# Sigmoid attention and top-1 mixture of experts: leftover rows gathered as quarters of a row and turned by VectorE

## The chip, the cores and the metric

One core of a Trainium2 chip. The metric is the device time of one execution in microseconds; a lower time is better. The time of the kernel before is the median of three runs. One execution was also profiled, and all rows of a profile come from that one.

## The reference, cut to what matters

```python
# q, k, v: (8, 12, 448, 64) fp32; w_gate (768, 8); w1 (8, 768, 1024); w2 (8, 1024, 768)
scores = q @ k.T / sqrt(64) - log(448)             # for each batch and head
x = (sigmoid(scores) @ v).transpose(0, 2, 1, 3).reshape(3584, 768)
logits = x @ w_gate
expert = argmax(logits, axis=1)                    # one of 8 experts for each row
gate = softmax(logits)[row, expert]
out[row] = gate * (relu(x[row] @ w1[expert]) @ w2[expert])
```

The kernel must give the output of shape (3584, 768) in fp32. Which rows go to which expert is known only when the attention has been computed.

## The kernel before, in words

**Stages.** The attention runs batch by batch and writes its rows to `x_tok` in memory. Seven *blocks* of 448 rows (0 to 6) each take one expert's weights through both layers (`moe`). The rows that such a block cannot hold are *leftover rows*. For them the attention stage writes *records* (row number, gate) to the memory array `recs`, in lists of 256 for one expert each. A list is an *item*. Two items always run, written out in full, behind block 6: item 0 and item 1 (`large`; in names of weights they carry the numbers 7 and 8). Further items run in a loop on the chip whose count comes from the data; in the profiled execution it takes no turn.

**Products.** Each fp32 operand is split in a high and a low part, and each product is made of three. A block has 144 products of 128x448 in the first layer (L231, eight steps j of 18) and 144 in the second (L254, six groups of 24). An item has as many, of 128x256: its first layer in L947, its second in L963. In the first layer ScalarE makes the hidden high part with a relu (`hh` in a block, `hih` in an item) and VectorE the low part (`hl`, `hil`). `ps_moe` has two PSUM banks, so the first product of step j + 2 waits for the low part of step j. In the second layer of a block, VectorE multiplies with the gate (L267) and turns the result (L268).

**Weights.** A raw tile `wst` is loaded by SP (five ahead). ScalarE casts it to the high part (`w1h`, `w2h`, L150), and GpSimd, or VectorE where `wts.low` says so, subtracts to get the low part (`w1l`, `w2l`, L151). First-layer parts have three buffers a kind, second-layer parts five.

**Leftover rows.** SP loads an item's records, 256 row numbers, two to a partition (L908). Two gathers on GpSimd's queue (L888) bring 128 whole rows each to `xg`. A row lies in `x_tok` as four quarters of six pieces of 32 elements; ScalarE copies it into six strips of four pieces, the order that the products need (`sort_rows`, L912). Then TensorE turns 128x128 pieces with an identity, four into one PSUM bank (L928), ScalarE casts to the high part (L932) and VectorE subtracts to get the low part (L933). Three calls of `split_rows` make an item's six *strips*, each a high and a low tile of 128x256 (`xrs_0`: `by_raw` and `rxf`; `xrs_1`: `rxh` and `rxl`).

**Order.** In this part the order on each engine is the order of the code. `mo` is a generator that issues block 6's products one by one; `more(n)` issues n of them and `until(n)` all but n, so the code between two such calls stands in the queues between those products. Item 0's products are stepped by `run` in the same way, and item 1's strips are made between its first steps.

Of the kernel before, what the change touches and what calls it, by code (L numbers as in the profile page):

```python
# [9 lines left out]
F32 = mybir.dt.float32  # L10
# [3 lines left out]
U32 = mybir.dt.uint32  # L14
AF = mybir.ActivationFunctionType
ALU = mybir.AluOpType
AX = mybir.AxisListType

P = 128
# [5 lines left out]
def tile_sigmoid_attention_top1_moe(  # L25
# [18 lines left out]
    nc = tc.nc  # L44
    B, H, S, D = q.shape
    NT, DM = out.shape
# [3 lines left out]
    KD = DM // P  # L50
# [7 lines left out]
    x_tok = dram.tile([NT, DM], F32, name="x_tok")  # L58
# [11 lines left out]
    ident = const.tile([P, P], F32, name="ident")  # L70
# [15 lines left out]
    TL = 2 * P  # L86
# [118 lines left out]
    def store():  # L205
        if stores:
            n, d, i, ob = stores.pop(0)
            cols = slice(d * DW + i * DW // 4, d * DW + (i + 1) * DW // 4)
            put = nc.sync.dma_start(
                out_b[bass.ds(maps[n], 1)][:, :, :, cols].rearrange("o r j f -> (o r) j f"),  # L210
                ob.rearrange("p j s t -> p j (s t)")[32 * i : 32 * (i + 1)],
            )
            apart(put, stored.setdefault((d, i), []))
# [571 lines left out]
    wts = Weights([(lambda b=b: regs.get(b)) for b in range(B + 1)])  # L785
# [8 lines left out]
    def more(n):  # L794
        nonlocal left
        for _ in range(min(n, left)):
            next(mo)
            left -= 1

    def until(n):  # L800
        more(left - n)
# [9 lines left out]
    rest = ctx.enter_context(tc.tile_pool(name="rest", bufs=1))  # L811
    ps_x = ctx.enter_context(tc.tile_pool(name="ps_x", bufs=2, space=bass.MemoryType.PSUM))
    ps_m2 = ctx.enter_context(tc.tile_pool(name="ps_m2", bufs=4, space=bass.MemoryType.PSUM))
    SMALL = P // 2

    xg = rest.tile([P, 2, DM], F32, name="xg")
    xgs = rest.tile([TS, DM], F32, name="xgs")
    xts_s = rest.tile([P, KD * TS], F32, name="xts_s")
    w1s = rest.tile([P, KD, DF], F32, name="w1s")
    w2s = rest.tile([P, KF, DM], F32, name="w2s")  # L820
# [21 lines left out]
    gate_e(NS - 1)  # L842
    more(9)
    nc.vector.tensor_sub(few, few, big)
    for cleared in (xg[:, 0], xg[:, 1], xgs):
        more(9)
        nc.vector.memset(cleared, 0.0)
    until(330)
# [27 lines left out]
    recs_v = recs.rearrange("(i t p) w -> i p t w", t=2, p=P)  # L876
    recs_s = recs.rearrange("(i r) w -> i r w", r=TL)
    recs_2 = [rest.tile([P, 2, 2], U32, name=f"rec_{n}") for n in range(3)]
    rec_s = rest.tile([TS, 1, 2], U32, name="rec_s")

    def item_reg(i):
        return nc.sync.value_load(li[0:1, bass.ds(i, 1)], min_val=0, max_val=NI - 1)

    def expert_reg(i):
        return nc.sync.value_load(li[0:1, bass.ds(i + P, 1)], min_val=0, max_val=E - 1)

    def gather(to, idx):
        nc.gpsimd.indirect_dma_start(  # L888
            out=to,
            out_offset=None,  # L890
            in_=x_tok,
            in_offset=bass.IndirectOffsetOnAxis(ap=idx, axis=0),
            bounds_check=NT - 1,
            oob_is_err=False,
        )
# [8 lines left out]
            oob_is_err=False,  # L904
        )

    def get_rows(ireg, rec):
        nc.sync.dma_start(rec, recs_v[bass.ds(ireg, 1)].rearrange("o p t w -> (o p) t w"))  # L908
        return [lambda t=t: gather(xg[:, t, :], rec[:, t, 0:1]) for t in range(2)]

    def sort_rows(to, frm):
        nc.scalar.copy(  # L912
            to.rearrange("p (k i s) -> p k i s", i=4, s=32), frm.rearrange("p (i k s) -> p k i s", i=4, s=32)
        )

    def sort_large(at, between=0):
        xp = [w2s[:, at + t] for t in range(2)]
        for t in range(2):
            sort_rows(xp[t], xg[:, t])
            more(between)  # L920
        return xp

    def split_rows(xp, xrs, k2):
        px = ps_x.tile([P, 512], F32, tag="px", name=f"px_{k2}")
        for kk in range(2):
            for t in range(2):
                at = kk * TL + t * P
                nc.tensor.transpose(px[:, at : at + P], xp[t][:, (2 * k2 + kk) * P : (2 * k2 + kk + 1) * P], ident)  # L928
        for kk in range(2):
            xh, xl = xrs[2 * k2 + kk]  # L930
            part = px[:, kk * TL : (kk + 1) * TL]
            nc.scalar.copy(xh, part)  # L932
            nc.vector.tensor_sub(xl, part, xh.bitcast(F32))  # L933

    def large(wts, b, rec, xrs, tags, home):

# [36 lines left out]
    def put_rows(xo, h, rec, puts):  # L973
        apart(scatter(xo[h], rec[:, h, 0:1]), puts)
# [8 lines left out]
    def small_rows(ireg):  # L983
        nc.sync.dma_start(rec_s, recs_s[bass.ds(ireg, 1), 0:TS].rearrange("o r (t w) -> (o r) t w", t=1))
        return [lambda: gather(xgs, rec_s[:, 0, 0:1])]

    def small_load(ereg, n):
        if n < KD:
            nc.sync.dma_start(w1s[:, n], w1[bass.ds(ereg, 1), n * P : (n + 1) * P, :].rearrange("e p n -> (e p) n"))
        else:  # L990
            j = n - KD
            nc.sync.dma_start(w2s[:, j], w2[bass.ds(ereg, 1), j * P : (j + 1) * P, :].rearrange("e p n -> (e p) n"))

    def yield_all(steps):
        while True:
            try:
                next(steps)
            except StopIteration as done:
                return done.value
# [3 lines left out]
    def small_item():  # L1003
# [51 lines left out]
    count = bass.RuntimeValue.of_register_unchecked(  # L1055
        bass.RegisterHandles([v_.val for v_ in loaded]), min_val=1, max_val=SMALL
    )
    gets = [get_rows(item_reg(n), recs_2[n]) for n in range(2)]
    regs[NS], regs[B] = expert_reg(0), expert_reg(1)
    more(24)  # L1060
    for get in gets[0]:
        get()
        more(12)
    more(36)
    by_raw = xpool.tile([P, S // 32, KD, 32], F32R, tag="raw", bufs=1, name="by_raw")
    by_raw = by_raw.rearrange("p j t s -> p (j t s)")
    first = [by_raw[:, n * TL : (n + 1) * TL] for n in range(2 * KD - 2)]
    first += [xpool.tile([P, S], F32R, tag="xf", bufs=6, name=f"rxf_{n}")[:, :TL] for n in range(2)]
    xrs_0 = [first[2 * t : 2 * t + 2] for t in range(KD)]
    xp_0 = sort_large(2, 12)  # L1070
    for get in gets[1]:
        more(12)
        get()
    for k2 in range(KD // 2):
        more(14)
        split_rows(xp_0, xrs_0, k2)
    more(24)
    xp_1 = sort_large(4, 12)
    until(24)
    wts.low = nc.vector  # L1080
    more(24)
    next(mo, None)
    xrs_1 = [
        [xpool.tile([P, S], F32R, tag=tag, name=f"r{tag}_{t}")[:, :TL] for tag in ("xh", "xl")] for t in range(KD)
    ]
    per_layer = 3 * KD * KF

    def run(steps, n):
        for _ in range(n):
            next(steps)  # L1090

    item = large(wts, NS, recs_2[0], xrs_0, (0, 2, 4), by_stores)
    for n in range(4):
        run(item, 20)
        store()
        if n < KD // 2:
            split_rows(xp_1, xrs_1, n)
    xo = yield_all(item)
    puts = []
    item = large(wts, B, recs_2[1], xrs_1, (6, 0, 2), by_stores)  # L1100
# [7 lines left out]
    with tc.If(count > 1, preferred_fallthrough_block=False):  # L1108
        with tc.For_i(1, count) as i, tc.manual_schedule():
            ereg, e_s = expert_reg(i + 1), expert_reg(i + SMALL - 1)  # L1110
            for get in get_rows(item_reg(i + 1), recs_2[2]) + small_rows(item_reg(i + SMALL - 1)):
                get()
            xp = sort_large(2)
            for k2 in range(KD // 2):
                split_rows(xp, xrs_1, k2)
            for n in range(KD + KF):
                small_load(e_s, n)
            ys = yield_all(large(Weights([lambda: ereg]), 0, recs_2[2], xrs_1, (0, 2, 4), by_hidden))
            for h in range(2):
                put_rows(ys, h, recs_2[2], [])  # L1120
            yield_all(small_item())
# [30 lines left out]
```

## Time and profile before

| | us |
|---|---|
| median of three runs | 781.88 (781.56 to 783.02) |
| time of the profiled execution | 784.5 |
| its span on the core | 782.7 |

| stretch of the span | from | to |
|---|---|---|
| block 6, first layer | 643.86 | 673.77 |
| block 6, second layer | 673.77 | 704.40 |
| item 0 | 704.40 | 740.24 |
| item 1 | 740.24 | about 775 |

The granted TensorE clock was 0.997 of full speed. PE is TensorE's products, PEld its weight loads, DVE is VectorE, ACT ScalarE, POOL GpSimd and SP the engine that issues most transfers. In a row of a timeline the first number is the start in microseconds, the second the duration, then engine, line, operation, output and inputs, shape, and the number of instructions that the row stands for; in brackets how long the engine idled before it and what released it. In a row of groups the numbers behind the bar are busy microseconds in all and mean nanoseconds of one. Names of tiles stand without their numbers.

### The profile page before, as it was taken

How to read it: one execution, taken by the hardware profiler on the slowest of the kernel's cores; microseconds unless marked ns; L12 is line 12 of the kernel's file. 1: busy time of each engine (PE TensorE's matmuls, PEld its weight loads, DVE VectorE, ACT ScalarE, POOL GpSimd, SP SyncE). 2: the span in 40 equal slices, each digit the busy share in tenths (PEclk: the TensorE clock that was granted, in tenths of full speed). 3: DMA queues.
4: the chain of work that ended last, by engine and by line, in shares of the span. 5: the costliest groups of instructions: out<-in, count | busy, mean ns of one | idle time of the engine just before them, and what ended most of it. 6: DMA issues, size and time to landing. Idle time of an engine off the chain costs nothing. (4 is left out here: it accounts for less than half of the span.)

```text
span 782.7 us, 15733 instructions
## 1 busy us (share of the span) xinstructions
PE 771.5 (99%) x5682; PEld 606.6 (78%) x5682; DVE 376.0 (48%) x811; ACT 384.9 (49%) x688; POOL 349.3 (45%) x331
## 2 busy tenths in 40 slices
PE   9999999999999999999999999999999999999996
PEld 5756556687686786867967769678688999999995
DVE  2354574375254652537425474244746492235443
ACT  5877675635536455264444552545523333435351
POOL 8747554152342332531615406054255755654341
PEclk9999999999999999999999999999999999999998
DMA  9776798975757847587576876766267555656661
GB/s 203 174 160 152 178 246 188 213 187 120 166 125 173 199 112 167 140 183 165 121 186 92 187 168 149 175 177 153 57 165 163 162 149 130 186 147 165 200 203 38
DMA packets 313683, 125.70 MB, mean 161 GB/s; under 512 B 210062, under 2 KB 311102, under 8 KB 313600
## 3 DMA queue, kind: packets, MB, share of 16 engines
q1 hardware_dynamic: 307552, 112.42, 61.5%
q0 software_dynamic: 5760, 11.76, 5.4%
q8 instruction: 47, 0.77, 0.4%
q10 hardware_dynamic: 288, 0.46, 0.2%
q14 instruction: 36, 0.29, 0.1%
HBM read 102.49 MB, written 22.49 MB: 160 GB/s over the span
## 5 line engine op out<-in xcount | busy, mean ns | idle before, releaser
L596 ACT ACTIVATE at<-sc,bias_s 128x448 f32<-128x448 f32 x336 | 193.4, 634 | 109.2 <-PE sc L610 108.1
L151 POOL TENSOR_TENSOR w1l<-wst,w1h 128x768 fp32r<-128x768 f32 x72 | 132.7, 1851 | 176.2 <-ACT w1h L150 161.7
L610 PE MATMUL sc<-qt,kt 64*64 64x448 f32 x1344 | 172.3, 546 | 1.1 <-ACT at L596 0.6
L627 PE MATMUL av<-at,vn 64*64 64x448 f32 x1344 | 168.6, 537 | 0.7 <-ACT xf L642 0.7
L151 POOL TENSOR_TENSOR w2l<-wst,w2h 128x512 fp32r<-128x512 f32 x84 | 106.9, 1298 | 138.6 <-ACT w2h L150 118.1
L610 PEld LDWEIGHTS sc<-qt,kt 64*64 64x64 f32 x1344 | 83.0, 189 | 56.1 <-issue 40.6
L231 PE MATMUL ps<-xh,w1h 128*128 128x448 f32 x336 | 124.3, 370 | 0.2 <-DVE nw L430 0.2
L231 PE MATMUL ps<-xh,w1l 128*128 128x448 f32 x336 | 123.4, 367 | 0.0
L231 PE MATMUL ps<-xl,w1h 128*128 128x448 f32 x336 | 123.3, 367 | 0.0
L254 PE MATMUL ps<-hh,w2l 128*128 128x448 f32 x336 | 123.3, 367 | 0.0
L254 PE MATMUL ps<-hl,w2h 128*128 128x448 f32 x336 | 123.2, 367 | 0.0
L254 PE MATMUL ps<-hh,w2h 128*128 128x448 f32 x336 | 122.7, 365 | 0.0
L627 PEld LDWEIGHTS av<-at,vn 64*64 64x64 f32 x1344 | 63.6, 133 | 59.9 <-issue 46.5
L150 ACT CAST w2h<-wst 128x512 fp32r<-128x512 f32 x108 | 64.6, 620 | 78.3 <-PE ps L254 64.5
L238 ACT ACTIVATE hh<-ps 128x448 fp32r<-128x448 f32 x56 | 30.6, 546 | 139.9 <-PE ps L231 139.9
L267 DVE TENSOR_TENSOR ps<-ps,gt 128x448 f32<-128x448 f32 x42 | 40.7, 969 | 85.9 <-PE ps L254 85.9
L486 DVE STREAM_TRANSPOSE xt<-av 128x448 f32<-128x448 f32 x48 | 28.5, 629 | 93.1 <-PE av L627 83.3
L239 DVE SCALAR_TENSOR_TENSOR hl<-ps,hh 128x448 fp32r<-128x448 f32 x56 | 34.4, 614 | 80.3 <-ACT hh L238 80.3
L231 PEld LDWEIGHTS ps<-xh,w1h 128*128 128x128 f32 x336 | 63.1, 188 | 9.9 <-issue 4.4
L254 PEld LDWEIGHTS ps<-hh,w2l 128*128 128x128 f32 x336 | 65.2, 194 | 6.6 <-issue 3.5
L254 PEld LDWEIGHTS ps<-hl,w2h 128*128 128x128 f32 x336 | 65.2, 194 | 6.2 <-issue 3.2
L254 PEld LDWEIGHTS ps<-hh,w2h 128*128 128x128 f32 x336 | 65.2, 194 | 3.4 <-DVE nw L430 0.2
(157 smaller groups left out, 953.8 us busy)
## 6 DMA issues: line engine op xcount, KB each, us to landing
wst<-in_moe_w_dram SPq DMA_DIRECT2D x72, 384.0 KB, 3.6
wst<-in_moe_w_dram SPq DMA_DIRECT2D x54, 512.0 KB, 5.0
x_tok<-xt SPq DMA_DIRECT2D x64, 168.0 KB, 2.9
qn<-in_q_dram SPq DMA_DIRECT2D x184, 56.0 KB, 3.5
raw<-x_tok SPq DMA_DIRECT2D x28, 336.0 KB, 8.1
out_dram<-ob SPq DMA_DIRECT2D x84, 112.0 KB, 2.3
kn<-in_k_dram SPq DMA_DIRECT2D x104, 56.0 KB, 4.4
kn<-in_k_dram POOLq DMA_DIRECT2D x80, 56.0 KB
```

What stands on the lines that cost most here:

```text
L150: nc.scalar.copy(hi, st)
L151: eng.tensor_tensor(lo, st, hi.bitcast(F32), op=ALU.subtract)
L231: nc.tensor.matmul(ps[:, :S], a[:, ws], b_, start=(t == 0 and n == 0), stop=(t == KD - 1 and n == 2))
L238: nc.scalar.activation(hh[:, :S], ps[:, :S], AF.Relu)
L239: nc.vector.scalar_tensor_tensor(hl[:, :S], ps[:, :S], 0.0, hh[:, :S].bitcast(F32), op0=ALU.max, op1=ALU.subtract)
L254: nc.tensor.matmul(ps[:, :S], a, b_, start=(j == 0 and n == 0), stop=(j == KF - 1 and n == 2))
L267: nc.vector.tensor_tensor(by_gate, by_gate, gate_rows[b], op=ALU.mult)
L486: nc.vector.transpose(xts[b][:, :, t, :], pv[:, :S].rearrange("p (j s) -> p j s", s=32))
L596: nc.scalar.activation(at, ps[:, :S], AF.Sigmoid, bias=bias_s, scale=SCALE)
L610: nc.tensor.matmul(ps[quarter(g, h), :S], ks, ops[g, "q"][OWN[h]], start=True, stop=True)
L627: nc.tensor.matmul(psv[g][OWN[h], :S], ops[g, "v"][rows, c, :], at[rows], start=(c == 0), stop=(c == KC - 1))
```

## The change

`x_tok` is seen as four times as many rows of 192 elements. A gather now brings 128 quarter rows: 32 rows, their four quarters in the four groups of 32 partitions. An item needs eight of them (`gather_quarters`, L915) in place of two gathers of whole rows. The index of a quarter is four times the row number plus the quarter's number; for that SP loads the row numbers four times, once for each group of partitions (L926), beside the record load that stays for the gate and the scatter (L930), and VectorE multiplies and adds (`place_rows`, L933, tile `at_q`). Rows that lie so need only a turn of blocks of 32x32 for a strip: one VectorE instruction into spare space of `w2s` (L942). ScalarE casts that to the high part (L944) and VectorE subtracts (L945), now with both inputs in SBUF. The 24 turning products and the four sorting copies of these two items are gone. `wts.low = nc.vector` stands earlier, so that all twelve second-layer low parts of block 6 are made by VectorE.

```diff
-    xg = rest.tile([P, 2, DM], F32, name="xg")
+    NB_I = TL // 32
+    xg = rest.tile([P, NB_I, KD, 32], F32, name="xg")
+    seg = rest.tile([P, 1], F32, name="seg")
+    for i in range(4):
+        nc.vector.memset(seg[32 * i : 32 * (i + 1)], float(i))
...
-    def get_rows(ireg, rec):
-        nc.sync.dma_start(rec, recs_v[bass.ds(ireg, 1)].rearrange("o p t w -> (o p) t w"))
-        return [lambda t=t: gather(xg[:, t, :], rec[:, t, 0:1]) for t in range(2)]
+    def gather_quarters(n, j):
+        nc.gpsimd.indirect_dma_start(
+            out=xg[:, j].rearrange("p t s -> p (t s)"),
...
+            in_=x_quarters,
+            in_offset=bass.IndirectOffsetOnAxis(ap=at_q[n][:, j : j + 1], axis=0),
...
+    def get_rows(ireg, n):
+        for i in range(4):
+            nc.sync.dma_start(
+                recs_q[n][32 * i : 32 * (i + 1)],
+                recs_s[bass.ds(ireg, 1)].rearrange("o (j r) w -> (o r) j w", r=32),
+            )
+        nc.sync.dma_start(recs_2[n], recs_v[bass.ds(ireg, 1)].rearrange("o p t w -> (o p) t w"))
+
+    def place_rows(n):
+        nc.vector.tensor_scalar(at_q[n], recs_q[n][:, :, 0], 4.0, seg, op0=ALU.mult, op1=ALU.add)
...
-    def split_rows(xp, xrs, k2):
-        px = ps_x.tile([P, 512], F32, tag="px", name=f"px_{k2}")
-        for kk in range(2):
-            for t in range(2):
-                at = kk * TL + t * P
-                nc.tensor.transpose(px[:, at : at + P], xp[t][:, (2 * k2 + kk) * P : (2 * k2 + kk + 1) * P], ident)
-        for kk in range(2):
-            xh, xl = xrs[2 * k2 + kk]
-            part = px[:, kk * TL : (kk + 1) * TL]
-            nc.scalar.copy(xh, part)
-            nc.vector.tensor_sub(xl, part, xh.bitcast(F32))
+    def split_rows(xrs, t):
+        whole = w2s[:, 2 + t, :TL]
+        nc.vector.transpose(whole.rearrange("p (j s) -> p j s", s=32), xg[:, :, t, :])
+        xh, xl = xrs[t]
+        nc.scalar.copy(xh, whole)
+        nc.vector.tensor_sub(xl, whole, xh.bitcast(F32))
...
-    gets = [get_rows(item_reg(n), recs_2[n]) for n in range(2)]
+    for n in range(2):
+        get_rows(item_reg(n), n)
     regs[NS], regs[B] = expert_reg(0), expert_reg(1)
     more(24)
-    for get in gets[0]:
-        get()
-        more(12)
+    wts.low = nc.vector
+    place_rows(0)
+    for j in range(NB_I):
+        more(5)
+        gather_quarters(0, j)
     more(36)
...
-    xp_0 = sort_large(2, 12)
-    for get in gets[1]:
-        more(12)
-        get()
-    for k2 in range(KD // 2):
-        more(14)
-        split_rows(xp_0, xrs_0, k2)
-    more(24)
-    xp_1 = sort_large(4, 12)
+    for t in range(KD):
+        split_rows(xrs_0, t)
+        more(8)
+    place_rows(1)
+    for j in range(NB_I):
+        more(5)
+        gather_quarters(1, j)
     until(24)
-    wts.low = nc.vector
...
         if n < KD // 2:
-            split_rows(xp_1, xrs_1, n)
+            split_rows(xrs_1, 2 * n)
+            split_rows(xrs_1, 2 * n + 1)
```

The same change stands in the loop for further items. Three places in the queues follow.

GpSimd's queue in block 6's first layer, before. `w1l_5` to `w1l_7` are the low parts for steps 5 to 7, `w2l_8` and on those of the second layer.

```order
L151 TENSOR_TENSOR w1l_5_7874<-wst_5_7620,w1h_5_7873 128x768
L888 DMA xg<-x_tok,rec_7765 128x768
L151 TENSOR_TENSOR w1l_6_7905<-wst_6_7640,w1h_6_7904 128x768
L888 DMA xg<-x_tok,rec_7765 128x768
L151 TENSOR_TENSOR w1l_7_7937<-wst_7_7668,w1h_7_7936 128x768
L151 TENSOR_TENSOR w2l_8_7943<-wst_8_7726,w2h_8_7942 128x512
```

The same queue now; `w1l_0` is item 0's first low part.

```order
L151 TENSOR_TENSOR w1l_5_7893<-wst_5_7625,w1h_5_7892 128x768
L915 DMA xg<-x_tok,at_q_7776 128x192 x2
L151 TENSOR_TENSOR w1l_6_7928<-wst_6_7645,w1h_6_7927 128x768
L915 DMA xg<-x_tok,at_q_7776 128x192 x3
L151 TENSOR_TENSOR w1l_7_7966<-wst_7_7673,w1h_7_7965 128x768
L915 DMA xg<-x_tok,at_q_7776 128x192 x3
L915 DMA xg<-x_tok,at_q_7777 128x192 x8
L151 TENSOR_TENSOR w1l_0_8275<-wst_0_8042,w1h_0_8274 128x768
```

Five gathers instead of two now stand ahead of `w1l_7`, and the second-layer low parts have left this queue.

VectorE's queue around the first gating of block 6's second layer, before. `hl_6` holds the low parts of steps 6 and 7.

```order
L239 SCALAR_TENSOR_TENSOR hl_6_8001<-ps_6_7_8014,hh_6_8000 128x448
L267 TENSOR_TENSOR ps_6_0_0_8037<-ps_6_0_0_8037,gt_7366 128x448
L268 STREAM_TRANSPOSE ob_0_8036<-ps_6_0_0_8037 128x448
L933 TENSOR_TENSOR by_raw<-px_8097,by_raw 128x256 x2
L267 TENSOR_TENSOR ps_6_0_1_8067<-ps_6_0_1_8067,gt_7366 128x448
```

The same place now.

```order
L942 STREAM_TRANSPOSE w2s<-xg 128x256
L945 TENSOR_TENSOR by_raw<-w2s,by_raw 128x256
L239 SCALAR_TENSOR_TENSOR hl_6_8035<-ps_6_7_8048,hh_6_8034 128x448
L942 STREAM_TRANSPOSE w2s<-xg 128x256
L945 TENSOR_TENSOR by_raw<-w2s,by_raw 128x256
L942 STREAM_TRANSPOSE w2s<-xg 128x256
L945 TENSOR_TENSOR by_raw<-w2s,by_raw 128x256
L942 STREAM_TRANSPOSE w2s<-xg 128x256
L945 TENSOR_TENSOR by_raw<-w2s,by_raw 128x256
L267 TENSOR_TENSOR ps_6_0_0_8076<-ps_6_0_0_8076,gt_7371 128x448
L268 STREAM_TRANSPOSE ob_0_8075<-ps_6_0_0_8076 128x448
```

One strip has moved ahead of the last `hl`, and three more stand between it and the first gating.

VectorE's queue in item 0's first layer, before. `psi_0` and `psi_1` are the sums of steps 0 and 1.

```order
L953 SCALAR_TENSOR_TENSOR hil_8330<-psi_0_8310,hih_8329 128x256
L933 TENSOR_TENSOR rxl_8299<-px_8343,rxh_8298 128x256
L933 TENSOR_TENSOR rxl_8301<-px_8343,rxh_8300 128x256
L953 SCALAR_TENSOR_TENSOR hil_8330<-psi_1_8339,hih_8329 128x256
L933 TENSOR_TENSOR rxl_8303<-px_8382,rxh_8302 128x256
```

The same place now.

```order
L965 SCALAR_TENSOR_TENSOR hil_8374<-psi_0_8354,hih_8373 128x256
L942 STREAM_TRANSPOSE w2s<-xg 128x256
L945 TENSOR_TENSOR rxl_8343<-w2s,rxh_8342 128x256
L942 STREAM_TRANSPOSE w2s<-xg 128x256
L945 TENSOR_TENSOR rxl_8345<-w2s,rxh_8344 128x256
L965 SCALAR_TENSOR_TENSOR hil_8374<-psi_1_8383,hih_8373 128x256
```

Each subtraction has got a turn ahead of it, and its input is `w2s` where it was the PSUM bank `px`.

More of the change, by code (lines that the diff above doesn't have):

```diff
@@ L844, in tile_sigmoid_attention_top1_moe @@
     nc.vector.tensor_sub(few, few, big)
-    for cleared in (xg[:, 0], xg[:, 1], xgs):
+    for cleared in (xg[:, : NB_I // 2], xg[:, NB_I // 2 :], xgs):
         more(9)
@@ L878, in tile_sigmoid_attention_top1_moe @@
     recs_2 = [rest.tile([P, 2, 2], U32, name=f"rec_{n}") for n in range(3)]
+    recs_q = [rest.tile([P, NB_I, 2], U32, name=f"rec_q{n}") for n in range(3)]
+    at_q = [rest.tile([P, NB_I], U32, name=f"at_q{n}") for n in range(3)]
+    x_quarters = x_tok.rearrange("n (i f) -> (n i) f", i=4)
     rec_s = rest.tile([TS, 1, 2], U32, name="rec_s")
@@ L905, in scatter @@
         )
-    def get_rows(ireg, rec):
-        nc.sync.dma_start(rec, recs_v[bass.ds(ireg, 1)].rearrange("o p t w -> (o p) t w"))
-        return [lambda t=t: gather(xg[:, t, :], rec[:, t, 0:1]) for t in range(2)]
+    def gather_quarters(n, j):
+        nc.gpsimd.indirect_dma_start(
+            out=xg[:, j].rearrange("p t s -> p (t s)"),
+            out_offset=None,
+            in_=x_quarters,
+            in_offset=bass.IndirectOffsetOnAxis(ap=at_q[n][:, j : j + 1], axis=0),
+            bounds_check=4 * NT - 1,
+            oob_is_err=False,
+        )
[4 more added lines that the diff above has]
+                recs_s[bass.ds(ireg, 1)].rearrange("o (j r) w -> (o r) j w", r=32),
+            )
+        nc.sync.dma_start(recs_2[n], recs_v[bass.ds(ireg, 1)].rearrange("o p t w -> (o p) t w"))
+    def place_rows(n):
+        nc.vector.tensor_scalar(at_q[n], recs_q[n][:, :, 0], 4.0, seg, op0=ALU.mult, op1=ALU.add)
     def sort_rows(to, frm):
@@ L914, in sort_rows @@
         )
-    def sort_large(at, between=0):
-        xp = [w2s[:, at + t] for t in range(2)]
-        for t in range(2):
-            sort_rows(xp[t], xg[:, t])
-            more(between)
-        return xp
-    def split_rows(xp, xrs, k2):
-        px = ps_x.tile([P, 512], F32, tag="px", name=f"px_{k2}")
-        for kk in range(2):
-            for t in range(2):
-                at = kk * TL + t * P
-                nc.tensor.transpose(px[:, at : at + P], xp[t][:, (2 * k2 + kk) * P : (2 * k2 + kk + 1) * P], ident)
-        for kk in range(2):
-            xh, xl = xrs[2 * k2 + kk]
-            part = px[:, kk * TL : (kk + 1) * TL]
-            nc.scalar.copy(xh, part)
-            nc.vector.tensor_sub(xl, part, xh.bitcast(F32))
+    def split_rows(xrs, t):
[4 more added lines that the diff above has]
+        nc.vector.tensor_sub(xl, whole, xh.bitcast(F32))
     def large(wts, b, rec, xrs, tags, home):
@@ L1110, in tile_sigmoid_attention_top1_moe @@
             ereg, e_s = expert_reg(i + 1), expert_reg(i + SMALL - 1)
-            for get in get_rows(item_reg(i + 1), recs_2[2]) + small_rows(item_reg(i + SMALL - 1)):
+            get_rows(item_reg(i + 1), 2)
+            place_rows(2)
+            for j in range(NB_I):
+                gather_quarters(2, j)
+            for get in small_rows(item_reg(i + SMALL - 1)):
                 get()
-            xp = sort_large(2)
-            for k2 in range(KD // 2):
-                split_rows(xp, xrs_1, k2)
+            for t in range(KD):
+                split_rows(xrs_1, t)
             for n in range(KD + KF):
```

## Prediction

> **What bounds the kernel now.** I read the page first, then the busy times by stretch over the part that changes, then each engine's timeline there.
>
> ```profile
> span 782.7 us, 15733 instructions
> PE 771.5 (99%) x5682; PEld 606.6 (78%) x5682; DVE 376.0 (48%) x811; ACT 384.9 (49%) x688; POOL 349.3 (45%) x331
> ```
> ```profile
> sum 131.00, PE 130.96 PEld 126.56 DVE 52.84 ACT 53.62 POOL 60.98; mean PE 32.74 PEld 31.64 DVE 13.21 ACT 13.41 POOL 15.25
> ```
>
> The sum is over 644 to 775 us: the last block (6), item 0 and item 1. TensorE idles 0.04 us of 131, so its queue is the clock: each product removed is time won, and each microsecond by which an operand comes too late is time lost, at once and in full. VectorE, ScalarE and GpSimd are under half busy, so only when their pieces end matters. I therefore walked the new order of every engine with the durations below and asked at each product of TensorE what is not there yet.
>
> **The gain.** Six groups of four turning products go.
>
> ```profile
> 678.05 0.37 PE L254 MATMUL ps<-hh,w2h 128*128 128x448 f32 x1
> 678.25 0.36 PE L254 MATMUL ps<-hl,w2h 128*128 128x448 f32 x1
> ...
> 681.71 0.36 PE L254 MATMUL ps<-hh,w2h 128*128 128x448 f32 x1
> 681.91 0.60 PE L928 MATMUL px<-ident,w2s 128*128 128x128 f32 x4
> 682.26 0.46 PE L254 MATMUL ps<-hl,w2h 128*128 128x448 f32 x1
> 682.56 0.36 PE L254 MATMUL ps<-hh,w2l 128*128 128x448 f32 x1
> ```
>
> From the product before a group (681.71) to the second behind it are 0.85 us; two pitches of 0.20 (first two rows) would be 0.41. A group costs 0.44, six cost **2.66 us**. The four sorting copies of ScalarE (0.83 each) lay in its idle time and give nothing.
>
> **Stall A: the eight gathers delay `w1l_7`.** Before, `w1l_6` and `w1l_7` had one gather ahead of each.
>
> ```profile
> 657.75 1.59 SPq L908 DMA_DIRECT2D rec<-recs  x2
> ```
> ```profile
> DMA to landing us min/median/max: 1.8/1.8/1.8
> ```
> ```profile
> 721.37 1.02 SPq L143 DMA_DIRECT2D wst<-in_moe_w_dram  x2
> ```
> ```profile
> 660.70 1.05 POOL L888 DMA_INDIRECT xg<-x_tok,rec  x1 [1.77 <-DVE hl L239]
> 661.77 1.86 POOL L151 TENSOR_TENSOR w1l<-wst,w1h 128x768 fp32r<-128x768 f32 x1
> 663.79 1.03 POOL L888 DMA_INDIRECT xg<-x_tok,rec  x1 [0.16 <-issue]
> 664.85 1.84 POOL L151 TENSOR_TENSOR w1l<-wst,w1h 128x768 fp32r<-128x768 f32 x1
> ...
> 674.15 1.02 POOL L888 DMA_INDIRECT xg<-x_tok,rec  x1
> 675.48 1.01 POOL L888 DMA_INDIRECT xg<-x_tok,rec  x1 [0.30 <-issue]
> ```
> ```profile
> 317.45 0.13 DVE L407 COPY rec<-gates 112x4 f32<-112x4 f32 x1
> ```
> ```profile
> 318.38 0.97 POOL L415 DMA_INDIRECT recs<-rec,si  x1 [2.93 <-DVE rec L407]
> ```
> ```profile
> 670.53 0.37 PE L231 MATMUL ps<-xh,w1l 128*128 128x448 f32 x1
> ```
>
> The records now come as four loads of 32 rows instead of one. Two plain issues of SP take 1.02, so 0.61 each with the tail; the fourth is issued 1.83 after the first (657.75), at 659.59. Landing takes at least 1.8; I take 2.06, the estimate that still leaves a wake-up of 0.80 before the gather at 660.70. So the records are there at 661.65. Now VectorE multiplies by 4 and adds the quarter (a small operation, 0.13 to 0.2): 661.85. A gather that waits for VectorE starts 0.80 after it (317.45 + 0.13 to 318.38): 662.65. Gather to gather is 1.33, gather to low part 1.06, low part to gather 0.16, a low part 1.85. Two gathers, `w1l_6`, three gathers, `w1l_7`: it starts at 670.79 and ends at 672.64 instead of 666.69, and TensorE wants it at 670.53. The old slack of 3.8 is gone; the stall is **2.1 us** (1.3 without the wake-up; 3.5 if SP needs 1.2 for each load, as in the 1.59 for two with their register work).
>
> **Stall B: the first pair of `item 0` stands ahead of block 6's last `hl`.** Gathers 6 to 8 go out behind `w1l_7`, at 672.80, 674.13 and 675.46. The turn needs all eight.
>
> ```profile
> q0 software_dynamic: 80, 0.39, 50.2%
> ```
> ```profile
> q0 software_dynamic: 80, 0.32, 18.3%
> ```
> ```profile
> 673.97 0.55 ACT L238 ACTIVATE hh<-ps 128x448 fp32r<-128x448 f32 x1 [1.34 <-PE ps L231]
> ```
> ```profile
> 674.55 0.62 DVE L239 SCALAR_TENSOR_TENSOR hl<-ps,hh 128x448 fp32r<-128x448 f32 x1 [3.02 <-ACT hh L238]
> ```
>
> The first two rows are the DMA queue of the gathers in 663.4 to 665.6 and in 665.6 to 670: the gather of 660.70 moved all its rows in the first, from 2.7 us after issue for about 2.1; that of 663.79 landed by 670. A quarter has a quarter of the bytes, 0.5. So a new gather lands 3.2 after issue, an estimate between 2.2 and 6.0 (663.79 to 670): 678.66. ScalarE's high part of the first strip stands ahead of the relu of j = 7, VectorE's turn and subtraction ahead of its `hl`: 0.40 + 0.37 + 0.55 + 0.60 = 1.92, at 680.58. TensorE wants that `hl` at 678.25 + 2.1 of stall A: **0.2 us** (0 to 2.6: microsecond for microsecond with the landing).
>
> The Trainium skill, page "DMA: Bandwidth & Descriptors", section "Anatomy of one DMA — SWDGE (gpsimd) path", puts such a transfer at about 2.0 us plus its bytes at 436 GB/s; by it a gather of 98 KB would land in an estimated 2.2 us and the sum would be about 1.0 lower, out of stalls B and C. The trace does not agree for the whole row: 2.9 us by that rule, 4.8 or more by the rows above.
>
> **Stall C: the strips in block 6's second layer.**
>
> ```profile
> L267 DVE TENSOR_TENSOR ps<-ps,gt 128x448 f32<-128x448 f32 x12 | 11.6, 966 | 19.6 <-PE ps L254 19.6
> L268 DVE STREAM_TRANSPOSE ob<-ps 128x448 f32<-128x448 f32 x12 | 7.8, 651 | 0.4
> ...
> L953 DVE SCALAR_TENSOR_TENSOR hil<-psi,hih 128x256 fp32r<-128x256 f32 x16 | 6.7, 420 | 12.9 <-ACT hih L952 12.9
> ...
> L933 DVE TENSOR_TENSOR rxl<-px,rxh 128x256 fp32r<-128x256 f32 x6 | 2.5, 425 | 3.2 <-ACT rxh L932 3.2
> ```
> ```profile
> L932 ACT CAST rxh<-px 128x256 fp32r<-128x256 f32 x6 | 2.2, 375 | 1.5 <-DVE rxl L933 1.5
> ```
>
> A strip is a turn (0.40, by size and a fixed part from L268's 0.65 at 448), a high part of 0.37 and a subtraction of 0.42, each waiting for the one before: 1.19. Three more strips now stand in VectorE's queue ahead of the first gating (0.97 + 0.65), the fifth ahead of `w2l_13`, the sixth ahead of `w2l_14`; ScalarE's high parts of the weights stand behind those of the strips. Walked from 680.58: `w2l_13` comes 0.2 late, `w2h_14` and `w2l_14` 0.45 and 0.3, and the second gating, behind them all, frees its bank 0.9 late: **1.85 us** (0.5 if the copies overlap better, 2.5 with the turns at the full 0.65).
>
> **Stall D: item 1's strips in item 0.** Two strips now stand between one `hil` and the next, three times.
>
> ```profile
> 708.16 0.42 DVE L933 TENSOR_TENSOR rxl<-px,rxh 128x256 fp32r<-128x256 f32 x1 [0.57 <-ACT rxh L932]
> ...
> 718.40 1.86 DVE L151 TENSOR_TENSOR w2l<-wst,w2h 128x512 fp32r<-128x512 f32 x1 [0.88 <-ACT w2h L150]
> ```
> ```profile
> 707.93 1.85 POOL L151 TENSOR_TENSOR w1l<-wst,w1h 128x768 fp32r<-128x768 f32 x1 [6.83 <-ACT w1h L150]
> ...
> 717.87 1.85 POOL L151 TENSOR_TENSOR w1l<-wst,w1h 128x768 fp32r<-128x768 f32 x1 [0.31 <-ACT w1h L150]
> ```
> ```profile
> 733.17 2.13 DVE L151 TENSOR_TENSOR w2l<-wst,w2h 128x512 fp32r<-128x512 f32 x3 [0.89 <-ACT w2h L150]
> ```
> ```profile
> 743.02 0.42 DVE L953 SCALAR_TENSOR_TENSOR hil<-psi,hih 128x256 fp32r<-128x256 f32 x1 [2.09 <-ACT hih L952]
> 745.18 0.42 DVE L953 SCALAR_TENSOR_TENSOR hil<-psi,hih 128x256 fp32r<-128x256 f32 x1 [1.74 <-ACT hih L952]
> ```
> ```profile
> 742.60 0.38 ACT L952 ACTIVATE hih<-psi 128x256 fp32r<-128x256 f32 x1 [5.82 <-PE psi L947]
> ```
> ```profile
> 743.79 1.84 POOL L151 TENSOR_TENSOR w1l<-wst,w1h 128x768 fp32r<-128x768 f32 x1 [0.43 <-ACT w1h L150]
> ```
>
> A low part on VectorE, both inputs in SBUF, takes 0.71 alone (2.13 for three) but 1.86 at 718.40, where GpSimd was in a low part until 719.72: it waited for its end. The old subtraction, one input in PSUM, ran its 0.42 inside GpSimd's 707.93 to 709.78. The new one has both inputs in SBUF. GpSimd's low part runs from 1.19 to 3.03 after a relu (742.60, 743.79). First strip after a relu: `hil` ends at 0.84, the turn 1.24, the high part 1.61; the subtraction waits for 3.03; then 0.42, the second strip 1.19, and the next `hil`, behind a relu that sits behind the second high part on ScalarE. From `hil` to `hil` that is about 4.05 us where TensorE's pitch is 2.16 (743.02 to 745.18). Two PSUM banks forgive the first 1.0; the rest is 0.86, 1.88 and 1.88, and `w2l_8` behind them 0.6: **5.2 us**. If the wait does not reach the subtraction, two strips of 1.19 and a `hil` of 0.42 are 2.8 against 2.16, and the banks take in nearly all: 0.6.
>
> The Trainium skill, page "SBUF — State Buffer", section "Who interferes with whom", states the same as a rule: a VectorE instruction with two SBUF inputs contends with a GpSimd instruction that reads SBUF, under an exclusive lock. By it the sum is the forecast, without it the first rival; the 1.86 against 0.71 agrees.
>
> **Costed at nothing.** The twelve second-layer low parts that move from GpSimd to VectorE are hidden in its idle half. Item 1's gathers follow on an empty GpSimd queue from about 690 and land before 706, ahead of their first turn near 708. SP's ten small loads push the raw second-layer weights back some 6 us; they still land at about 671.5, and no product waits for them. Four one-column memsets early on are below 1 us of idle VectorE.
>
> **The sum:** 2.1 + 0.2 + 1.85 + 5.2 − 2.66 = **+6.7 us**. On the profiled execution's 784.5 that is 791.2; the runs shown have the median 781.88, 2.6 lower, so I forecast **788.6**.
>
> **Rivals.** (1) *GpSimd does not hold the subtractions up.* For it: the rows of the wait are of 128x512, not 128x256. Against: the wait ended with GpSimd's instruction, whatever the size. Stall D is 0.6: +2.1, 784.0. (2) *All is hidden, the other side.* The walk's stalls A and B hang on issue times: if `w1l_7` is done by 670.53 (2.1 earlier, say with records after 1.8 and no wake-up), the gathers landed 2.2 after issue, and D without the wait, only the gain stays: −2.66, 779.2. The point that decides first is 670.53. Against: five gathers at 1.33 plus two low parts are 9.6 us behind a start that cannot be before 660.7. (3) *Gathers land late.* 4.5 to 6.0 after issue, as whole rows did: B grows by 1.3 to 2.8, to +9.5 or 791.4.
>
> **Chances.** Forecast 0.48, rival 3 0.16, both slower. Rival 1 0.24, of which 0.08 ends within 0.2% (1.56 us, about what a measurement of this kernel tells from no change) and 0.16 slower. Rival 2 0.12, 0.10 faster and 0.02 the same. So faster 0.10, same 0.10, slower 0.80. The range reaches down past rival 1's lower end (no wait, quick landings: −0.4), and up to rival 3 with the longer SP issues: 781.5 to 792.5. The forecast's own range is 786 to 791.
>
> **What would show it.** Right: a gap of about 2 us on TensorE near 671 before a product of `w1l`, small ones before `hl` near 680 and between 686 and 692, gaps of 1 to 2 us before three first products of item 0's first layer, and L945 at 1.0 to 1.8 us there instead of 0.42. Wrong: L945 at 0.42 throughout, `w1l_7` ending before 671, or a TensorE without gaps. Any gap in item 1 would be a cost that I have not seen.

## The result and the profile after

The changed kernel takes 792.74 us (median of four runs, 791.4 to 794.51) against 781.74: a ratio of 1.0132, 95% interval 1.0118 to 1.0147, or 9.2 to 11.5 us slower. The time lies 0.2 us above the top of the range, and the loss is larger than the 6.7 forecast. The profiled execution has 792.93 us and a span of 790.9.

The page's first line, and the sum of busy times over 644 to 783 us, the stretch that answers to 644 to 775 before:

```profile
span 790.9 us, 15757 instructions
```
```profile
sum 139.00, PE 131.62 PEld 123.64 DVE 69.87 ACT 50.45 POOL 59.14; mean PE 32.90 PEld 30.91 DVE 17.47 ACT 12.61 POOL 14.78
```

TensorE idled 0.04 us of this stretch before; now it idles 7.4. Its timeline shows where. These are the products behind a gap of more than 0.3 us; the bracket gives the idle time and what ended it.

```profile
672.33 0.47 PE L231 MATMUL ps<-xh,w1l 128*128 128x448 f32 x1 [1.15 <-POOL w1l L151]
...
680.58 0.48 PE L254 MATMUL ps<-hh,w2h 128*128 128x448 f32 x1 [0.46 <-ACT hh L238]
...
681.24 0.48 PE L254 MATMUL ps<-hl,w2h 128*128 128x448 f32 x1 [0.18 <-DVE hl L239]
...
689.89 0.48 PE L254 MATMUL ps<-hh,w2h 128*128 128x448 f32 x1 [0.22 <-ACT w2h L150]
...
693.59 0.46 PE L254 MATMUL ps<-hh,w2h 128*128 128x448 f32 x1 [0.66 <-DVE ob L268]
...
715.63 0.51 PE L959 MATMUL psi<-by_raw,w1h 128*128 128x256 f32 x2 [0.67 <-DVE hil L965]
...
719.63 0.50 PE L959 MATMUL psi<-by_raw,w1h 128*128 128x256 f32 x2 [1.58 <-DVE hil L965]
...
723.63 0.51 PE L959 MATMUL psi<-by_raw,w1h 128*128 128x256 f32 x2 [1.58 <-DVE hil L965]
```

The bracket leaves out the tail of the product before. Counted from start to start and less the usual pitch, the gaps are 1.31, 0.63, 0.46, 0.39, 0.83, 0.83, 1.74 and 1.74; with two of 0.2 in block 6's second layer, 8.3 us. Each stands within 2 us of where one of the four stalls was placed, with a releaser that the prediction named; only the gap before `hh` at 680.58 had no term of its own in the sum.

GpSimd's queue at stall A, now:

```profile
661.92 1.05 POOL L915 DMA_INDIRECT xg<-x_tok,at_q  x1 [2.81 <-DVE at_q L933]
663.27 1.01 POOL L915 DMA_INDIRECT xg<-x_tok,at_q  x1 [0.31 <-issue]
664.32 1.85 POOL L151 TENSOR_TENSOR w1l<-wst,w1h 128x768 fp32r<-128x768 f32 x1
666.33 1.30 POOL L915 DMA_INDIRECT xg<-x_tok,at_q  x1 [0.16 <-issue]
...
670.44 1.83 POOL L151 TENSOR_TENSOR w1l<-wst,w1h 128x768 fp32r<-128x768 f32 x1
...
675.35 1.01 POOL L915 DMA_INDIRECT xg<-x_tok,at_q  x1 [0.30 <-issue]
```

`w1l_7` ends at 672.27, where it ended at 666.69 before, and TensorE starts behind it. VectorE's first turn waits for the last of these gathers:

```profile
679.20 0.45 DVE L942 STREAM_TRANSPOSE w2s<-xg 128x256 f32<-128x256 f32 x1 [5.76 <-DMA xg<-x_tok,at_q]
```

The subtractions by group, all shapes apart (busy microseconds in all, mean nanoseconds of one):

```profile
L945 DVE TENSOR_TENSOR rxl<-w2s,rxh 128x256 fp32r<-128x256 f32 x6 | 6.1, 1010 | 2.8 <-ACT rxh L944 2.8
L945 DVE TENSOR_TENSOR by_raw<-w2s,by_raw 128x256 fp32r<-128x256 f32 x5 | 2.1, 425 | 2.4 <-ACT by_raw L944 2.4
```

The same instruction takes 0.425 us in block 6, where GpSimd runs no low part, and 1.01 in the mean in item 0, where it does: three of the six take 1.6. Each of these three starts while GpSimd is in a low part and ends 0.3 us behind it. The first, and GpSimd's low part:

```profile
712.38 1.61 DVE L945 TENSOR_TENSOR rxl<-w2s,rxh 128x256 fp32r<-128x256 f32 x1 [0.47 <-ACT rxh L944]
```
```profile
711.86 1.85 POOL L151 TENSOR_TENSOR w1l<-wst,w1h 128x768 fp32r<-128x768 f32 x1 [5.04 <-ACT w1h L150]
```

What I had not seen is the end. The last product starts at 774.68 before and at 781.93 after, 7.25 later, but the span is 8.2 longer and the median 11.0. The last scatter, on GpSimd, of before and of after:

```profile
775.76 0.98 POOL L898 DMA_INDIRECT out_dram<-xo,rec  x1 [1.88 <-DVEq L1108]
```
```profile
785.26 0.98 POOL L905 DMA_INDIRECT out_dram<-xo,rec  x1 [4.13 <-issue]
```

It starts 1.08 us after the last product before and 3.33 after it now. After's chain of work that ended last names the reason, in order of time:

```profile
780.13 3.06 DMA out_dram<-xo,rec
```

GpSimd waits for the landing of the scatter before it, just ahead of the loop for further items, which takes no turn. A software transfer is one that GpSimd issues, such as a gather or a scatter, and its landing is told by a completion semaphore, a counter that an engine can wait for. There are eight of them, DMASW0 to DMASW7. In the program, GpSimd's wait at the loop names six before, and not that of the scatter just issued (DMASW3); now it names all eight, that of this scatter (DMASW7) among them:

```
before: L1108 ISA [waits Pool_49,DMASW5_49,DMASW6_49,DMASW4_49,DMASW7_49,DMASW1_49,DMASW0_49]
after:  L1121 ISA [waits Pool_49,DMASW4_49,DMASW5_49,DMASW3_49,DMASW6_49,DMASW2_49,DMASW7_49,DMASW1_49,DMASW0_49]
```

The loop's body holds six software transfers before (three gathers, three scatters) and twelve now. They are dealt out to the eight semaphores in turn, so the body now uses every one. In the trace the wait for DMASW7 ends at 783.2, when the scatter of 780.13 has landed.

### The profile page after: what moved, and what is told of

It is laid out like the page before. It is cut to its first block, busy times and chain, and to the rows that moved or that the text cites. A ratio compares the mean times of both kernels' runs of the same rounds, so it can differ in the third digit from the quotient of the medians.

```text
span 790.9 us, 15757 instructions
## 1 busy us (share of the span) xinstructions
PE 772.0 (98%) x5658; PEld 602.5 (76%) x5658; DVE 393.2 (50%) x841; ACT 380.8 (48%) x684; POOL 347.8 (44%) x331
## 5 line engine op out<-in xcount | busy, mean ns | idle before, releaser
L610 PE MATMUL sc<-qt,kt 64*64 64x448 f32 x1344 | 168.4, 546 | 1.1 <-ACT at L596 0.6
L627 PE MATMUL av<-at,vn 64*64 64x448 f32 x1344 | 164.8, 537 | 0.9 <-ACT xf L642 0.9
L151 POOL TENSOR_TENSOR w2l<-wst,w2h 128x512 fp32r<-128x512 f32 x72 | 91.6, 1296 | 127.6 <-ACT w2h L150 109.9
L610 PEld LDWEIGHTS sc<-qt,kt 64*64 64x64 f32 x1344 | 80.6, 189 | 56.1 <-issue 41.9
L627 PEld LDWEIGHTS av<-at,vn 64*64 64x64 f32 x1344 | 61.7, 133 | 61.0 <-issue 48.1
```

The source lines that it names most:

```text
L151: eng.tensor_tensor(lo, st, hi.bitcast(F32), op=ALU.subtract)
L610: nc.tensor.matmul(ps[quarter(g, h), :S], ks, ops[g, "q"][OWN[h]], start=True, stop=True)
L627: nc.tensor.matmul(psv[g][OWN[h], :S], ops[g, "v"][rows, c, :], at[rows], start=(c == 0), stop=(c == KC - 1))
```

## The experiments

The kernel before took 781.58 to 781.95 us in the comparisons below.

**The tail: the kernel before with two idle gathers (`t_before`).** Only the body of the loop that takes no turn is written differently.

```diff
-            for get in get_rows(item_reg(i + 1), recs_2[2]) + small_rows(item_reg(i + SMALL - 1)):
+            gets_2 = get_rows(item_reg(i + 1), recs_2[2])
+            for get in gets_2 + gets_2 + small_rows(item_reg(i + SMALL - 1)):
                 get()
```

> The kernel before with two gathers more in the loop that takes no turn (each of its two gathers is written twice); nothing that runs is changed. Theory of the tail: GpSimd now waits at the loop for the landing of the scatter just issued, the last scatter starts about 3.3 us after the last product, and the kernel takes 783.7 to 784.7. Rival (code that does not run costs nothing): 781.7.

784.74 us against 781.58, ratio 1.0045 (1.0031 to 1.0059): 3.2 us slower, with one instruction more that runs (15734 instead of 15733): a wait for semaphores at the loop. Its last product starts at 774.06, its last scatter 3.21 later:

```profile
777.27 0.98 POOL L898 DMA_INDIRECT out_dram<-xo,rec  x1 [4.01 <-issue]
```

So the tail is real. The scatter's start moved by 2.1 us against the last product, the median by 3.2 (interval 2.4 to 4.6). What makes up the difference isn't shown: behind the start of the last scatter the span runs on for 5.6 us here, for 4.9 in `again` and for 5.6 in `t_after` below.

**The tail from the other side (`t_after`).** In the changed kernel's loop, `get_rows` to `split_rows` are those of before.

```diff
...
-            get_rows(item_reg(i + 1), 2)
-            place_rows(2)
-            for j in range(NB_I):
-                gather_quarters(2, j)
-            for get in small_rows(item_reg(i + SMALL - 1)):
+            for get in get_whole(item_reg(i + 1), recs_2[2]) + small_rows(item_reg(i + SMALL - 1)):
                 get()
...
-            for t in range(KD):
-                split_rows(xrs_1, t)
...
+            for k2 in range(KD // 2):
+                split_whole(xp, xrs_1, k2)
```

> The changed kernel, but the loop for further items, which takes no turn, has the two whole-row gathers and the turning products of the kernel before. Theory of the tail (the loop holds so many gathers that GpSimd, before it passes the loop, waits for every software transfer, also for the scatter that it has just issued): the last scatter starts 1.1 us after the last product instead of 3.3 and the kernel takes 789.7 to 790.7. Rival (the tail is noise of single executions, all of the loss is stalls of TensorE): 792.7, and the last scatter as late as before.

789.93 us, ratio 1.0113 (1.0098 to 1.0129), 2.8 less than the changed kernel. Its gaps are those of the changed kernel, 8.1 us in all. The last product starts at 780.55 and the scatter 1.08 later:

```profile
781.63 0.98 POOL L905 DMA_INDIRECT out_dram<-xo,rec  x1 [1.88 <-DVEq L1139]
```

**Again the kernel before (`again`).**

> The kernel before, unchanged, for a second profile of it: the time is 781.6, and from the last product to the end of the span it shows how far the 8.0 us of the first profile are typical. Theory of the tail (the wait at the loop costs about 3 us in the median, of which the first profiles showed only 1.0 because that of before ended late): about 5 to 6 us here. Rival: 8 us here too.

781.61 us, ratio 0.9999 (0.999 to 1.0008). From its last product (775.02) to the end of the span (781.0) it is 6.0 us, against 8.0 in the first profile and 9.0 in the changed kernel's. The other kernels without the wait at the loop have 6.5 (`best1`, below) and 6.7 (`t_after`), those with it 8.7 to 9.0 (`t_before` has 8.8). So the first profile of before ended late by 1.3 to 2 us, and hid much of the tail when span was set against span.

**Stall D: turns into PSUM (`d_psum`).** Item 1's strips alone.

```diff
-    def split_rows(xrs, t):
-        whole = w2s[:, 2 + t, :TL]
+    def split_rows(xrs, t, low=False):
+        whole = ps_x.tile([P, 512], F32, tag="px", name=f"px_{t}")[:, :TL] if low else w2s[:, 2 + t, :TL]
...
-            split_rows(xrs_1, 2 * n)
-            split_rows(xrs_1, 2 * n + 1)
+            split_rows(xrs_1, 2 * n, True)
+            split_rows(xrs_1, 2 * n + 1, True)
```

> Only item 1's strips are changed: VectorE turns them into a PSUM bank instead of spare SBUF, so that the subtraction has one input in PSUM again. Theory (GpSimd's low part holds up a VectorE subtraction with two SBUF inputs): the six subtractions of L945 in item 0 take 0.42 us each, where three of them took 1.6; TensorE's gaps there fall from 4.6 us to at most 1.3, and the kernel takes about 788.9 us (3.3 to 4.3 less than the changed kernel's 792.7). Rival (it is the two turns in VectorE's queue that delay the next low part, whatever their memory): gaps and time stay, 792.7.

789.08 us, ratio 1.01 (1.0085 to 1.0116), 3.7 less than the changed kernel. The group of subtractions and the one gap of more than 0.3 us that is left in item 0:

```profile
L945 DVE TENSOR_TENSOR rxl<-px,rxh 128x256 fp32r<-128x256 f32 x6 | 2.5, 425 | 2.6 <-ACT rxh L944 2.6
```
```profile
718.70 0.51 PE L959 MATMUL psi<-by_raw,w1h 128*128 128x256 f32 x2 [0.37 <-DVE hil L965]
```

No subtraction is held up, though all six still start while GpSimd is in a low part, and the gaps in item 0 fall from 4.3 to 0.8 us with the same number of turns at the same places. The memory of the input, not the count of instructions, made 3.5 of the 4.3 us of stall D.

**Stall D: one strip behind each step (`d_spread`).**

```diff
-    for n in range(4):
-        run(item, 20)
-        store()
-        if n < KD // 2:
-            split_rows(xrs_1, 2 * n)
-            split_rows(xrs_1, 2 * n + 1)
+    for n in range(KD):
+        run(item, 20 if n == 0 else 18)
+        if n % 2 == 0:
+            store()
+        split_rows(xrs_1, n)
+    store()
```

> The changed kernel, with item 1's strips one behind each of six steps of item 0 instead of two behind each of three; still turned in SBUF. Theory (each subtraction waits for the end of GpSimd's low part, and two strips behind one relu are more than a step can hold): subtractions of L945 still take 1.0 to 1.6 us, but the two PSUM banks absorb one wait per step, the three gaps of 0.8, 1.7 and 1.7 go, one of up to 1.6 us comes near step 7 where the second-layer low parts start: 789.5 to 790.5. Rival (the number of strips does not matter, the wait does): six waits of 1.2 show, 793 or more.

790.9 us (788.07 to 792.27), ratio 1.0121 (1.0106 to 1.0137): 1.8 less than the changed kernel, where 2.2 to 3.2 were expected, and the two intervals do not tell them apart. So the time settles nothing here. Its profiled execution, the fastest, shows the expected picture: the gaps in item 0 fall from 4.3 to 1.15 us, four of the six subtractions are still held up (1.0 to 1.6 us), and one gap is left, near the last step.

```profile
L945 DVE TENSOR_TENSOR rxl<-w2s,rxh 128x256 fp32r<-128x256 f32 x6 | 5.5, 912 | 2.8 <-ACT rxh L944 2.8
```
```profile
723.61 0.50 PE L959 MATMUL psi<-by_raw,w1h 128*128 128x256 f32 x2 [0.99 <-DVE hil L965]
```

In that execution the same wait costs TensorE little where there is one for each step: the banks take it in. What the slower executions of this kernel add was not profiled.

**Stalls A to C: gathers 28 products later (`a_late`).**

```diff
     place_rows(0)
+    more(28)
     for j in range(NB_I):
```

> All eight gathers of item 0 are issued 28 products later, behind w1l_7; what follows in block 6 moves back by as many products. Theory (gathers ahead of w1l_7 and strips ahead of the last hl make stalls A and B): the gaps before the product with w1l_7 (1.3) and before hh and hl at 680 (1.1) are gone; some of it comes back at the later gatings, up to 2 us, since the strips now crowd there: 789.5 to 792. Rival (the delay is that of the new gathers' landing, wherever they stand): the sum of gaps in block 6 stays at 4.7 and the time at 792.7.

791.68 us, ratio 1.0131 (1.0116 to 1.0147): 1.1 below the changed kernel, which the two intervals do not tell apart. The profile says why. The gaps at 672 and 680 are gone; a new one of 0.35 stands at 662.63, behind a `hl` that stood behind the index operation in VectorE's queue. That one took 1.36 us instead of 0.23: it started while GpSimd was in `w1l_6` and ended with it. But the strips now crowd ahead of a gating, and its bank comes late by 2.40 us:

```profile
690.72 0.45 PE L254 MATMUL ps<-hh,w2h 128*128 128x448 f32 x1 [2.24 <-DVE ob L268]
```

Behind that gap the granted clock (third number from the right) halved. The busy times of 691.8 to 695:

```profile
691.80:695.00 3.20, 3.20 (x10) 2.85 (x10) 2.69 (x6) 1.21 (x3) 1.24 (x2) 0.54 0.25 53
```

Ten products in 3.2 us where there would be 15.8 at a pitch of 0.2025: 1.2 us more. A and B were saved and given back there.

**Undo one part: low parts back on GpSimd (`c_low`).** `wts.low = nc.vector` stands where it stood before.

```diff
-    wts.low = nc.vector
     place_rows(0)
...
     until(24)
+    wts.low = nc.vector
     more(24)
```

> The changed kernel with one part undone: the twelve second-layer low parts of block 6 stay on GpSimd, behind the gathers. Theory (a queue of gathers at 1.3 us each delays all behind it): stall A stays 1.3, low parts w2l_8 to w2l_11 come 1.5 to 2 us late twice and those behind item 1's eight gathers about 5 us late: 799 to 801. Rival (GpSimd is less than half busy and has room for them): 791 to 793.

801.27 us, ratio 1.0249 (1.0234 to 1.0265), 8.5 more than the changed kernel. The products that wait for second-layer low parts behind the gathers:

```profile
677.45 0.48 PE L254 MATMUL ps<-hh,w2l 128*128 128x448 f32 x1 [1.14 <-POOL w2l L151]
...
704.17 0.74 PE L254 MATMUL ps<-hh,w2l 128*128 128x448 f32 x1 [3.94 <-POOL w2l L151]
```

So this part of the change is what keeps the loss from being 19.5 us instead of 11.0. GpSimd's mean load (45% busy over the whole span before) says nothing of a queue of sixteen gathers at 1.3 us.

**All together (`best1`, and once more as `best1b`).** The turning products stay away, and each cause is taken out: gathers behind `w1l_7`, item 1's into spare `w1s`; turns in PSUM, two turns ahead of two subtractions, behind the gatings; the loop of `t_after`.

```diff
-        whole = w2s[:, 2 + t, :TL]
...
+    def split_rows(frm, xrs, ts):
+        turned = []
+        for t in ts:
+            whole = ps_x.tile([P, 512], F32, tag="px", name=f"px_{t}")[:, :TL]
...
+        for t, whole in zip(ts, turned):
+            nc.vector.tensor_sub(xrs[t][1], whole, xrs[t][0].bitcast(F32))
...
+    until(196)
+    for n in range(2):
+        for j in range(NB_I):
+            gather_quarters(n, j)
+            more(2)
...
+    until(94)
+    split_rows(xg, xrs_0, (0, 1))
+    until(70)
+    split_rows(xg, xrs_0, (2, 3))
+    until(46)
+    split_rows(xg, xrs_0, (4, 5))
...
+    until(22)
+    split_rows(xg_1, xrs_1, (0, 1))
...
+    run(item, 20)
+    store()
+    split_rows(xg_1, xrs_1, (2,))
```

(and one strip more behind each of the next three steps of 18 products).

> The change with its stalls designed away: gathers of both items behind w1l_7 (item 1's into a buffer of their own, inside the unused w1s), turns into PSUM, two strips at a time with both turns ahead of both subtractions, placed behind a gating or behind a step of item 0, and whole-row gathers in the loop that takes no turn. Theory (the losses are the stalls A to D and the wait at the loop): no gap of TensorE is left but for a few tenths, the last scatter starts 1.1 us after the last product, and the 2.66 us of the turning products are a gain: 779.0, ratio 0.996 to 0.998. Rival (the new gathers or turns cost something wherever they stand): 781.5 or more.

780.97 us against 781.73: ratio 1.0 (0.9984 to 1.0016), with three of eleven times between 783.1 and 786.4. The range of the expectation was missed. Its profile has no gap from block 6 to the end, and its last product starts at

```profile
772.45 0.28 PE L997 MATMUL psi<-w2h,hil 128*128 128x256 f32 x1
```

which is 2.57 ahead of the 775.02 of `again`. The profiles reach block 6 at slightly different times; from its first product to the last of item 1 it is 128.2 us here, and 130.8, 130.9 and 130.9 in the three profiles of kernels with the turning products and without stalls (the first, `again`, `t_before`): 2.6 to 2.7 less, the turning products' 2.66.

> The version without stalls once more, unchanged, since its first comparison left open whether it beats the kernel before (780.97 against 781.73, interval 0.9984 to 1.0016) though its profile has its last product 2.6 us earlier. Theory (only the gain is left): 779.5 to 780.5, ratio 0.997 to 0.999. Rival (something that a single profile does not show takes the gain back in some executions): 781 or more, with single times far above the rest as the first time.

780.41 us against 781.95: ratio 0.9978 (0.9966 to 0.9989), 1.5 us faster, with a last product at 773.39 in its profile, 128.7 behind block 6's first, and no gap. So of two comparisons of one program, one shows it 0.2% faster, clear of noise, and the other no difference. Why the median shows 0.8 and 1.5 of the 2.6 us stays open; single executions lie far above the rest, and none of those was profiled.

## Why the prediction was right, and where it was short

**The gain** (2.66). Right: 2.6 to 2.7 us from block 6's first product to the last one in `best1`, about 2.1 in `best1b`.

**Stall A** (2.1). The mechanism is right, the size 1.31. The records landed a little sooner, at_q began at 661.41, and the first gather followed the index by 0.3 us instead of the 0.80 taken from the scatter rows: it started at 661.92, not 662.65. Half of these 0.73 us was lost again in the queue (from 666.33 the next gather came after 1.60, where 1.33 was taken), so `w1l_7` ended 0.37 sooner than forecast. The rest of the difference is TensorE's: its products lay 2% further apart ahead of the stall (see the last section), and it was ready for `w1l_7` at 671.02, not at 670.53.

**Stall B** (0.2). Right in place, too small: 0.46 before `hl`, and 0.63 before `hh`, which had no term. The gathers landed 3.85 us after issue (675.35 to 679.20), where the sum had 3.2. The estimate of 2.2 us worked out from the Trainium skill's page "DMA: Bandwidth & Descriptors", section "Anatomy of one DMA — SWDGE (gpsimd) path", does not agree with this.

**Stall C** (1.85). 0.20, 0.39, 0.21 and 0.83: 1.63.

**Stall D** (5.2). 0.83, 1.74 and 1.74: 4.31. The three gaps came within 0.15 of the walk; the 0.6 for `w2l_8` did not come. That GpSimd holds the subtractions up is shown by `d_psum` and by their ends, 0.3 us behind GpSimd's; that a VectorE instruction with two SBUF inputs contends with a GpSimd instruction that reads SBUF is the rule that the page "SBUF — State Buffer" of the Trainium skill states in its section "Who interferes with whom": the trace agrees, with 1.6 us against 0.425. Rival 1 is out; so are rival 2, since `w1l_7` was done at 672.27, and rival 3, since the gathers landed 3.85 after issue and not 4.5 or more.

**What the sum lacked.** Stalls of 9.35 were forecast and 8.3 measured, so the walk was not short there. The step that failed is the list of what costs nothing: it ended at TensorE's last product and took the tail as unchanged, and the gathers in the loop as code that does not run. That term was 0 and is about 3 us (3.2 in `t_before`, 2.8 in `t_after`). A smaller one is the restart: behind a gap the second product starts 0.1 late as well, nine times, about 1 us in all. With these, 8.3 − 2.7 + 3.0 + 1.0 = 9.6, inside the measured 9.2 to 11.5. The medians are 11.0 apart; of the 1.4 us that are missing, some 0.4 is the wider spacing of the products told in the last section, in the profiled execution at least, and the rest stays without a cause.

The last product came 7.25 later, close to the forecast of 6.7, and that is in part luck: stalls forecast 1.0 too large in all stand against restarts and a spacing of the products that no term held.

**The anchor.** I set the sum against a profile of 784.5 and the runs' 781.88, and did not ask where those 2.6 us were. Some 1.3 to 2 of them were in the tail.

## What to carry to other kernels

Where one engine is full and the others half empty, walk each queue instruction by instruction: it gave the place of all four stalls here, and their sizes within a microsecond. Moving work from the full engine to an idle one pays only if its pieces end in time; look at what stands behind them in the queue, and at the memory that their inputs lie in when another engine is at work there. Continue the walk to the last instruction of the program, and count transfers also in code that does not run: they set what is waited for at the loop.

## What the runs showed of the hardware

- A VectorE subtraction of 128x256 with both inputs in SBUF takes 1.6 us instead of 0.425 when it starts while GpSimd is in a subtraction from SBUF: it ends 0.3 us behind GpSimd's. With one input in PSUM it takes 0.425 there (`d_psum`).
- The index operation (L933, one array of 128x8 and a column of scalars, all in SBUF) was held up in the same way: 1.36 us in `a_late` and in `best1`, where it ended with GpSimd's low part, and 0.23 where GpSimd was idle.
- After a gap of 2.40 us on TensorE the granted clock fell to 0.54 for 3.2 us (`a_late`); the gap of 4.1 us in `c_low` was followed by 0.51 to 0.57 for 3.8 us. After the gaps of 1.74 in the changed kernel the granted clock stayed at 1.00. The Trainium skill's page "TensorE: Matmul & The Clock Gate", section "Part 1: The HAM clock gate", puts the idle time that throttles at about 3.4 us; 2.4 was enough here.
- From 651 to 671 us, with no gap, the changed kernel's profile has 98 products and that of before 101, both at a granted clock of 1.00. The busy times of that stretch, before and after:

```profile
651.00:671.00 20.00, 20.00 (x101) 1.00 0.66 187
```
```profile
651.00:671.00 20.00, 20.00 (x98) 1.00 0.54 126
```

  From start to start a product takes 0.2067 us in the one and 0.2027 in the other, some 0.4 us in this stretch. It isn't the change: `best1b`, the same program as `best1`, has 0.207 from 651 to 661 where `best1` has 0.203. What makes it is not known.
